# Forty-eight products of ones among the early steps, k as the first transfer, and softmax sums in a PSUM tile of their own

## The chip, the cores and the metric

The kernel runs on one core of one Trainium2 chip. The metric is the device time of one execution in microseconds (us). Timed runs of the kernel before gave 588.23, 587.32 and 587.64, median 587.64.

The engines are TensorE (PE, with its weight loads as PEld), VectorE (DVE), ScalarE (ACT) and GpSimd (POOL). SyncE (SP) issues all transfers from HBM. Each engine works through its own list in order; between engines there are semaphores.

## The reference

Attention of 4 batches, 8 heads, 768 positions and a head dimension of 64: each query sees the keys within 15 positions and one summary for each block of 32 keys (the maximum of its keys, the mean of its values). Its output goes through an MLP from 512 to 2048 and back, with an exact gelu.

```python
k_sum = k.reshape(B, H, nb, block, D).max(axis=3)
v_sum = v.reshape(B, H, nb, block, D).mean(axis=3)
scores_l = scale * np.matmul(q, k.transpose(0, 1, 3, 2))
scores_l_m = np.where(mask_l, scores_l, -1000000000.0)
scores_s = scale * np.einsum('bhsd,bhnd->bhsn', q, k_sum) + np.log(block)
scores_all = np.concatenate([scores_l_m, scores_s], axis=-1)
a = np.exp(scores_all - np.max(scores_all, axis=-1, keepdims=True))
a = a / (np.sum(a, axis=-1, keepdims=True) + 1e-09)
attn_out = np.matmul(a, np.concatenate([v, v_sum], axis=2))
x = attn_out.transpose(0, 2, 1, 3).reshape(B * S, H * D)
h = x @ w_in
out = (0.5 * h * (1.0 + erf(h / np.sqrt(2.0)))) @ w_out
```

The weights are drawn in 64-bit and come in as raw 64-bit words.

## The kernel before

The attention is cut into 24 units of 4 heads and 256 queries; two units make a chunk of 256 tokens with all 512 columns of x. Units 0 to 5 compute in f32, the later ones in f16 with a high and a low part. Chunks 0 and 1 go through `phase1` (x times w_in, three f16 products for each) and `phase2` (times w_out); from chunk 2 on groups of chunks share sums and differences, so that fewer products are needed.

What every engine does, and in which order, stands in one string, `ORDER`: some 1,670 named steps, each with its numbers. The program goes through it and issues each step's instructions; every engine gets its part in this order, and the transfers of the `fetch_` and `load_` steps go to SP in this order too. The string is at the head of the file; its first line names the steps of the first microseconds.

The steps that matter here, with their lines in the trace:

- `setup` (L325): GpSimd sets constants; `ones` is 128 x 64 of 1.0. TensorE multiplies `ones` with itself 16 times (`N_FILL`, L331) into a tile of the pool `ps_h` that nobody reads.
- `fetch_k 0 g` (L496) brings k for two pairs of heads of batch 0 (784 KB); `prep_k` (L505) takes the block maxima on VectorE, `prep_k_end` (L513, L514) splits them, `k_pack` (L633, L635) lays k and the maxima out on ScalarE.
- `load_q u` (L577) brings q of unit u into the only q tile. The first in the string is that of unit 6, which `s_q_hi` (ScalarE, L682) and `q_lo` (VectorE, L691) split at once; `load_q 0` has to wait until they have read it.
- `f_mask` (L620) writes the mask into the scores' tile by f16 products, `f_scores` (L649) adds q times k in f32, `evac` (ScalarE, L727) copies the scores, `maximum` (GpSimd, L740) takes the maximum over partitions, `m_shift` (L697) subtracts it by products with one row, `m_exponent` (ScalarE, L703) applies the exponential. The scores have one PSUM tile (`ps_s`, two banks), so the next unit's `f_mask` waits for `m_exponent`.
- `f_sums` (L671) sums the exponentials by products with ones, `norm_take` (VectorE, L814) transposes the sums out of PSUM, `norm_cross` (ScalarE, L822, L827), `norm_rec` (L830) and `norm_spread` (L834) make the factors. `f_values` (L663) multiplies with v, `norm_mult` (VectorE, L841) applies the factors, `x_hi` (L845) and `x_lo` (L848) split x for the MLP. Sums and values share one tile of two banks, `psv`: values in its first bank, sums in its second. There is one such tile, and waits are kept for a tile as a whole. `sums` and `values` are the f16 forms of the later units.
- `fetch_w_in`, `wi_bits` (L372, L377, L381), `wi_hi` (ScalarE, L407), `wi_lo` (VectorE, L410) and `wt_add` turn the 64-bit words of w_in into f16 parts. `sum_vt` (L532) and `mean_vt` make the means of v for batch 0.
- `phase1 c i` (L868 to L870): 24 products for chunk c and 256 columns i of w_in, into a tile of `ps_h` (three tiles).

Of the kernel before, what the change touches and what calls it, by code (L numbers as in the profile page):

```python
# [77 lines left out]
sum_vt 0, wi_bits 5 0, wt_add 3 1, wt_add 3 2, wi_lo 3, load_v 0, wi_hi 2, wt_hi 3, evac 1, maximum 1, fetch_vt 2,
wi_bits 5 1, wt_lo 3, load_q 2, sum_vt 1, norm_take 0, norm_cross 0, k_pack 2, m_shift 1, m_exponent 1, sum_vt 2,
norm_rec 0, norm_spread 0, wi_bits 6 0, wi_bits 5 2, wi_bits 6 1, wi_lo 2, wi_hi 5, mean_vt, s_load_vs 0, wi_bits 6 2,  # L80
fetch_w_in 4 4, wi_lo 5, f_mask 2, f_scores 2, evac 2, wi_bits 4 0, wi_bits 4 1, maximum 2, load_v 1, s_load_vs 1,
f_values 0, norm_mult 0, x_hi 0, fetch_w_in 0 0, k_pack 3, f_sums 1, norm_take 1, x_lo 0, load_v 2, norm_cross 1,
wi_bits 4 2, m_shift 2, load_q 3, f_values 1, wi_bits 0 0, m_exponent 2, norm_rec 1, norm_spread 1, f_mask 3,
norm_mult 1, wi_bits 0 1, wi_hi 4, f_scores 3, fetch_w_in 1 1, x_hi 1, x_lo 1, wi_bits 0 2, wi_bits 1 0, evac 3,
fetch_v 1 1, f_sums 2, phase1 0 3, wi_hi 0, wi_hi 6, norm_take 2, fetch_w_in 7 3, wi_bits 1 1, load_k 4, wi_lo 6,
load_vs 2, prep_v 1 1, f_values 2, fetch_k 1 3, norm_cross 2, phase1 0 2, k_sums 0 0, norm_rec 2, norm_spread 2,
phase1 0 5, load_v 3, wi_bits 1 2, fetch_k 1 1, gelu 0 3, norm_mult 2, maximum 3, m_shift 3, wi_hi 1, load_v 4,
m_exponent 3, wi_lo 0, prep_k 1 3, phase1 0 6, gelu 0 5, wi_lo 1, wi_bits 7 0, load_vs 3, prep_k 1 1, f_sums 3,
norm_take 3, wi_bits 7 1, fetch_k 1 2, x_hi 2, f_values 3, load_q 4, prep_k 1 2, gelu 0 2, g_hi 0 3, fetch_v 1 2, g_lo
0 3, g_hi 0 2, norm_cross 3, norm_rec 3, g_hi 0 5, phase1 0 0, x_lo 2, k_pack 4, fetch_k 1 0, norm_spread 3, norm_mult  # L90
3, x_hi 3, phase1 0 1, gelu 0 1, fetch_v 1 0, wi_bits 7 2, g_lo 0 5, g_hi 0 1, x_lo 3, load_vs 4, f_mask 4, f_scores
4, wi_hi 7, evac 4, gelu 0 6, prep_k 1 0, maximum 4, wi_lo 7, phase1 1 3, prep_v 1 2, f_mask 5, prep_v 1 0, g_lo 0 2,
g_hi 0 6, gelu 1 3, g_lo 0 1, g_lo 0 6, load_k 5, fetch_w_out 1 5, wo_bits 1 0, k_pack 5, shift 4, fetch_w_out 0 4,
load_k 6, phase1 1 7, g_hi 1 3, wo_bits 1 1, phase1 0 7, gelu 1 7, g_hi 1 7, g_lo 1 7, exponent 4, wo_bits 1 2, gelu 0
7, wo_bits 0 0, wo_bits 0 1, wo_bits 0 2, load_q 5, phase1 1 1, gelu 0 0, g_hi 0 0, f_sums 4, g_hi 0 7, f_values 4,
gelu 1 1, wo_hi 1, g_lo 0 0, norm_take 4, f_scores 5, norm_cross 4, g_lo 0 7, phase1 1 6, g_hi 1 1, evac 5, wo_lo 1,
gelu 1 6, s_k_hi 6, fetch_w_out 3 5, wi_lo 4, norm_rec 4, load_q 7, load_v 6, phase1 1 2, norm_spread 4, norm_mult 4,
fetch_w_out 2 4, g_lo 1 3, phase1 1 4, maximum 5, wo_hi 0, wo_lo 0, f_mask 6, gelu 1 2, phase1 1 5, load_mask, k_lo 6,
fetch_v 1 3, shift 5, load_v 5, exponent 5, prep_k_end 1 0, load_k 8, wo_bits 3 0, g_lo 1 1, wo_bits 3 1, phase1 1 0,
gelu 1 0, g_hi 1 2, prep_v 1 3, wo_bits 3 2, phase2 0 0, g_hi 1 6, k_sums 1 0, load_vs 5, gelu 1 5, g_hi 1 5, f_sums  # L100
5, wo_hi 3, wo_bits 2 0, g_lo 1 2, norm_take 5, wo_bits 2 1, phase1 0 4, s_q_hi 7, x_hi 4, wo_bits 2 2, wo_hi 2, wo_lo
3, load_vs 6, q_lo 7, scores 6, s_k_hi 8, wo_lo 2, prep_k_end 1 1, fetch_w_out 5 5, f_values 5, k_sums 0 1, k_lo 8,
x_lo 4, phase2 0 1, norm_cross 5, evac 6, maximum 6, norm_rec 5, norm_spread 5, norm_mult 5, fetch_w_out 4 4, phase2 0
3, gelu 1 4, wo_bits 5 0, v_hi 6, wo_bits 5 1, f_mask 7, x_hi 5, x_lo 5, g_hi 1 4, g_lo 1 4, gelu 0 4, g_lo 1 5,
phase2 0 2, phase1 2 4, wo_bits 4 0, g_lo 1 6, gelu 2 4, phase1 2 1, wo_bits 4 1, wo_bits 4 2, load_v 8, load_k 7,
s_k_hi 7, phase1 2 0, g_hi 0 4, wo_hi 4, gelu 2 1, load_q 8, wo_bits 5 2, wo_hi 5, shift 6, wo_lo 4, load_vs 8, phase1
2 2, fetch_w_out 7 5, g_hi 1 0, g_lo 0 4, wo_lo 5, s_q_hi 8, gelu 2 0, g_lo 1 0, phase2 0 4, exponent 6, s_p_hi 6,
k_lo 7, phase1 2 6, v_lo 6, fetch_w_out 6 4, k_sums 1 1, scores 7, q_lo 8, v_hi 8, p_lo 6, gelu 2 6, sums 6, wo_bits 7
0, wo_bits 6 0, wo_bits 7 1, load_k 9, wo_bits 6 1, wo_bits 6 2, values 6, s_k_hi 9, evac 7, phase2 0 5, phase1 2 7,
wo_bits 7 2, wo_hi 6, wo_lo 6, wo_hi 7, fetch_k 2 3, load_q 9, g_hi 2 0, load_v 7, load_vs 7, wo_lo 7, k_lo 9, scores  # L110
8, norm_take 6, add_mask 8, phase2 0 6, norm_cross 6, norm_rec 6, norm_spread 6, s_q_hi 9, g_hi 2 1, phase2 0 7, store
0 0, maximum 7, v_lo 8, q_lo 9, shift 7, exponent 7, s_p_hi 7, phase2 1 0, norm_mult 6, load_q 11, s_q_hi 11, phase2 1
2, g_hi 2 4, phase2 1 4, wt_add 4 0, put 0 0, prep_k 2 3, p_lo 7, sums 7, v_hi 7, store 0 1, fetch_v 2 0, v_lo 7,
wt_add 4 1, wt_add 4 2, load_v 9, put 0 1, load_k 11, load_vs 9, g_lo 2 4, g_hi 2 6, norm_take 7, g_lo 2 1, g_lo 2 0,
prep_v 2 0, maximum 8, x_hi 6, phase2 1 6, gelu 2 2, phase1 2 5, norm_cross 7, norm_rec 7, x_lo 6, store 1 0, shift 8,
scores 9, gelu 2 7, q_lo 11, exponent 8, values 7, fetch_v 2 2, wt_hi 4, phase2 1 1, norm_spread 7, wt_lo 4, phase2 1
3, phase2 1 5, add_mask 9, prep_v 2 2, norm_mult 7, load_q 10, phase2 1 7, load_v 11, g_hi 2 2, s_q_hi 10, s_p_hi 8,
s_k_hi 11, load_vs 11, p_lo 8, sums 8, values 8, v_hi 9, v_lo 9, maximum 9, shift 9, fetch_k 2 1, k_lo 11, prep_k 2 1,
g_hi 2 7, g_lo 2 7, scores 11, exponent 9, put 1 0, x_hi 7, phase1 2 3, norm_take 8, load_k 10, x_lo 7, phase1 3 7,
g_lo 2 6, q_lo 10, gelu 2 5, load_v 10, add_mask 11, norm_cross 8, norm_rec 8, fetch_k 2 2, s_p_hi 9, norm_spread 8,  # L120
p_lo 9, s_k_hi 10, phase1 3 5, gelu 2 3, norm_mult 8, store 1 1, gelu 3 5, prep_k 2 2, prep_k_end 2 1, sums 9,
norm_take 9, x_hi 8, phase2 2 1, k_lo 10, scores 10, fetch_k 2 0, put 1 1, values 9, maximum 11, g_hi 2 3, g_lo 2 3,
g_hi 2 5, norm_cross 9, shift 11, exponent 11, wt_add 5 0, s_p_hi 11, load_vs 10, load_k 12, norm_rec 9, norm_spread
9, phase1 3 4, load_q 12, s_q_hi 12, g_lo 2 5, gelu 3 7, v_hi 10, phase1 3 0, gelu 3 4, v_hi 11, g_hi 3 4, norm_mult
9, g_lo 2 2, phase2 2 3, x_hi 9, wt_add 1 0, phase1 3 3, wt_add 1 1, wt_add 1 2, p_lo 11, g_hi 3 5, q_lo 12, wt_hi 1,
add_mask 10, sums 11, gelu 3 3, v_lo 11, g_hi 3 3, prep_k 2 0, phase2 2 5, load_v 12, g_lo 3 4, fetch_v 2 1, phase1 3
6, norm_take 11, wt_add 5 1, norm_cross 11, g_lo 3 3, k_sums 2 1, prep_k_end 2 0, k_sums 2 0, load_q 13, gelu 3 0,
s_q_hi 13, wt_lo 1, s_k_hi 12, q_lo 13, k_lo 12, wt_add 5 2, wt_hi 5, phase1 3 1, prep_v 2 1, v_lo 10, phase2 2 7,
store 2 1, scores 12, load_k 13, wt_lo 5, phase1 3 2, maximum 10, shift 10, wt_add 0 0, values 11, s_k_hi 13, load_q
14, s_q_hi 14, phase2 2 0, phase2 2 2, wt_add 2 0, g_hi 3 0, norm_rec 11, norm_spread 11, exponent 10, s_p_hi 10,  # L130
norm_mult 11, g_lo 3 0, phase2 2 4, g_lo 3 5, wt_add 0 1, p_lo 10, values 10, wt_add 2 1, wt_add 0 2, x_lo 8, wt_hi 0,
# [1165 lines left out]
```

## Time and profile before

| | us |
|---|---|
| median of three runs | 587.64 |
| lowest and highest | 587.32 and 588.23 |
| the profiled execution's own time | 588.54 |
| its span, first to last instruction | 586.8 |
| TensorE busy (share of the span) | 568.8 (97%) |
| VectorE busy | 459.2 (78%) |
| ScalarE busy | 386.5 (66%) |
| GpSimd busy | 87.5 (15%) |

The span is that of the instructions; 1.7 us of the profiled execution's time lie around it. Busy time is the union of an engine's instructions. Matmuls overlap in the array and their ends are modelled, so a busy TensorE need not be one at its peak. The granted clock is the share of TensorE's 2.4 GHz that it was allowed in a stretch; it has two levels here, 0.50 and 1.00.

### The profile page before, as it was taken

How to read it: one execution, taken by the hardware profiler on the slowest of the kernel's cores; microseconds unless marked ns; L12 is line 12 of the kernel's file. 1: busy time of each engine (PE TensorE's matmuls, PEld its weight loads, DVE VectorE, ACT ScalarE, POOL GpSimd, SP SyncE). 2: the span in 40 equal slices, each digit the busy share in tenths (PEclk: the TensorE clock that was granted, in tenths of full speed). 3: DMA queues.
4: the chain of work that ended last, by engine and by line, in shares of the span. 5: the costliest groups of instructions: out<-in, count | busy, mean ns of one | idle time of the engine just before them, and what ended most of it. 6: DMA issues, size and time to landing. Idle time of an engine off the chain costs nothing.

```text
span 586.8 us, 13450 instructions
## 1 busy us (share of the span) xinstructions
PE 568.8 (97%) x5784; PEld 392.8 (67%) x5784; DVE 459.2 (78%) x621; ACT 386.5 (66%) x648; POOL 87.5 (15%) x42
## 2 busy tenths in 40 slices
...
GB/s 290 328 245 279 165 209 292 194 168 131 147 146 167 82 42 159 100 116 121 75 85 75 85 133 4 56 99 79 74 62 1 20 19 19 1 18 2 2 1 91
DMA packets 28652, 64.27 MB, mean 110 GB/s; under 512 B 2736, under 2 KB 7600, under 8 KB 28592
## 3 DMA queue, kind: packets, MB, share of 16 engines
...
q8 instruction: 45, 0.74, 0.5%
...
## 4 chain that ended last, share of the span: by engine, by line
PE 92%; ACT 2%; POOL 2%; DMA 2%; DVE 2%; issue 1%; POOLq 0%; DVEq 0%; ACTq 0%
PE psy L939 13%; PE pso L987 12%; PE pso L989 11%; PE pso L988 11%; PE psz L939 7%; PE psh L868 5%; PE psh L869 5%; PE psh L870 5%; PE pso_y L1152 4%; PE psx L939 3%; PE pss L649 3%; PE psv L793 3%; PE pss L716 2%; PE pss_x L1152 2%; POOL m L740 2%; DMA q<-in_qd_dram 2%
## 5 line engine op out<-in xcount | busy, mean ns | idle before, releaser
L740 POOL PARTITION_ALL_REDUCE m<-s x24 | 81.3, 3386 | 331.9 <-DVE s L731 113.0
L987 PE MATMUL pso<-w_out_h,gg 128*128 128x512 f16 x320 | 121.5, 380 | 0.0
L988 PE MATMUL pso<-w_out_l,gg 128*128 128x512 f16 x320 | 121.3, 379 | 0.0
L989 PE MATMUL pso<-w_out_h,gg 128*128 128x512 f16 x320 | 121.3, 379 | 0.0
L939 PEld LDWEIGHTS <-wt 128*128 128x128 f16 x768 | 74.5, 98 | 13.6 <-issue 0.8
L868 PE MATMUL psh<-xos,ww 128*128 128x256 f16 x256 | 70.9, 277 | 0.0
L869 PE MATMUL psh<-xos,ww 128*128 128x256 f16 x256 | 70.8, 277 | 0.0
L870 PE MATMUL psh<-xos,ww 128*128 128x256 f16 x256 | 70.8, 276 | 0.0
L939 PE MATMUL psy<-xos,wt 128*128 128x256 f16 x576 | 69.3, 273 | 0.0
L939 PEld LDWEIGHTS <-ww 128*128 128x128 f16 x576 | 55.1, 98 | 11.8 <-issue 0.6
L989 PEld LDWEIGHTS <-gg 128*128 128x128 f16 x320 | 31.3, 98 | 37.8
L987 PEld LDWEIGHTS <-gg 128*128 128x128 f16 x320 | 31.3, 98 | 33.7 <-issue 1.5
L988 PEld LDWEIGHTS <-gg 128*128 128x128 f16 x320 | 31.3, 98 | 31.6
L950 ACT ACTIVATE ww<-psy 128x512 f32<-128x512 f32 x48 | 28.1, 590 | 31.1 <-PE psy L939 30.8
L971 DVE SCALAR_TENSOR_TENSOR gg<-g,gg 128x512 f16<-128x512 f32 x48 | 34.8, 731 | 13.4 <-ACT gg L967 13.4
L957 DVE TENSOR_TENSOR g<-psz,ww 128x512 f32<-128x512 f32 x24 | 16.4, 685 | 20.3 <-PE psz L939 17.6
L967 ACT ACTIVATE gg<-g 128x512 f16<-128x512 f32 x48 | 29.3, 623 | 3.2 <-PE pso L988 2.6
L877 ACT ACTIVATE g<-psh 128x512 f32<-128x512 f32 x32 | 18.8, 594 | 16.8 <-PE psh L870 14.5
L868 PEld LDWEIGHTS <-ww 128*128 128x128 f16 x256 | 25.4, 99 | 6.2 <-issue 2.0
L964 ACT ACTIVATE g<-g 128x512 f32<-128x512 f32 x36 | 22.2, 622 | 8.8 <-DVE g L957 8.8
L869 PEld LDWEIGHTS <-ww 128*128 128x128 f16 x256 | 25.4, 99 | 3.8
L870 PEld LDWEIGHTS <-ww 128*128 128x128 f16 x256 | 25.4, 99 | 3.3
...
## 6 DMA issues: line engine op xcount, KB each, us to landing
...
```

The costliest lines, as they stand in the source:

```text
L740: nc.gpsimd.partition_all_reduce(out_ap=self.m32, in_ap=self.s32, channels=P, reduce_op=bass_isa.ReduceOp.max)
L868: nc.tensor.matmul(ph[:, e, :], wh, xh, start=(k == 0), stop=False)
L869: nc.tensor.matmul(ph[:, e, :], wh, xl, start=False, stop=False)
L870: nc.tensor.matmul(ph[:, e, :], wl, xh, start=False, stop=(k == NCC - 1))
L939: nc.tensor.matmul(ps[:, e, :], ws, xx, start=(first and e == 0 and k == 0 and m == 0), stop=(k == 1 and m == 2), skip_group_check=True,)
L950: nc.scalar.activation(snaps[b, q, n], split8(acc[b, q, "y"]), AF.Copy)
L967: nc.scalar.activation(g_part(o // 2, q, 0, slice(o % 2, 4, 2)), g32t[b, q, o], AF.Copy, scale=SC_G)
L971: nc.vector.scalar_tensor_tensor(out=g_part(o // 2, q, 1, fs), in0=g32t.pop((b, q, o)), scalar=SC_G, in1=g_part(o // 2, q, 0, fs), op0=ALU ...
L987: nc.tensor.matmul(p, gh, w_out_h[:, f, :], start=(f == 0), stop=False)
L988: nc.tensor.matmul(p, gh, w_out_l[:, f, :], start=False, stop=False)
L989: nc.tensor.matmul(p, gl, w_out_h[:, f, :], start=False, stop=(f == NFC - 1))
L1152: nc.tensor.matmul(ps[:, j, :], g, ww_, start=(first and e == 0 and k == 0), stop=(e == 1 and k == 2), skip_group_check=True,)
```

## The change

Four things are changed; the order of all other steps stays.

A new step `fill k` multiplies `ones` with itself six times into a tile of `ps_h` of its own, as `setup` does 16 times. Eight such sets stand in the string: 7 and 0 behind `f_mask 0`, 4, 3, 2 and 1 behind `f_scores 0`, 6 and 5 behind `f_sums 1`. `fetch_k 0 0` moves from the fifth place of the string to the first, ahead of `load_q 6`. The tile of two banks for values and sums is parted: values get a tile of one bank (`ps_v`), sums one of half a bank (`ps_d`), each with waits of its own. `v_tile` makes a new tile at each call instead of reusing the unit's.

```diff
+N_FILL_STEP = 6
...
-load_q 6, s_q_hi 6, q_lo 6, load_m16, fetch_k 0 0, prep_k 0 0, fetch_w_in 3 3, f_mask 0, load_q 0, prep_k_end 0 0,
+fetch_k 0 0, load_q 6, s_q_hi 6, q_lo 6, load_m16, prep_k 0 0, fetch_w_in 3 3, f_mask 0, fill 7, fill 0, load_q 0,
...
+    ps_d = ctx.enter_context(tc.tile_pool(name="ps_d", bufs=1, space=PSUM))
...
+    def products_of_ones(name, n):
+        t = ps_h.tile([P, DM], F32, tag="psh", name=f"psh_fill_{name}")
+        for _ in range(n):
+            nc.tensor.matmul(
+                t[:D].rearrange("p (n d) -> p n d", d=D), ones, ones.unsqueeze(1).broadcast_to([P, DM // D, D]),
+                start=True, stop=True,
+            )
+
+    def fill(k):
+        products_of_ones(k, N_FILL_STEP)
...
-            self.pss = self.psv = None
+            self.pss = None
...
-                            self.psv[e * D : (e + 1) * D, 0, col], v[:, vo : vo + D], self.s32[:, po : po + TQ],
+                            self.psv[e * D : (e + 1) * D, col], v[:, vo : vo + D], self.s32[:, po : po + TQ],
...
         def f_sums(self):
-            self.v_tile()
+            self.d_tile()
...
-                    self.psv[i * 32 : (i + 1) * 32, 1, :CH], ones_f, self.s32[:, i * CH : (i + 1) * CH],
+                    self.psd[i * 32 : (i + 1) * 32], ones_f, self.s32[:, i * CH : (i + 1) * CH],
...
         def v_tile(self):
-            if self.psv is None:
-                self.psv = ps_v.tile([P, 2, NR * CH], F32, tag="psv", name=f"psv_{self.nm}")
+            self.psv = ps_v.tile([P, NR * CH], F32, tag="psv", name=f"psv_{self.nm}")
+
+        def d_tile(self):
+            self.psd = ps_d.tile([P, CH], F32, tag="psd", name=f"psn_{self.nm}")
...
-            nc.vector.transpose(out=self.dent[:, :CH], in_=self.psv[:, 1, :CH])
+            nc.vector.transpose(out=self.dent[:, :CH], in_=self.psd)
```

On SP, at the program's start, before: q of unit 6, the mask, k, the bits of w_in 3, q of unit 0.

```order
L577 DMA q_6_123<-in_qd_dram 128x512
L317 DMA mask_sb<-in_mask_dram 128x320
L496 DMA w_out_l<-in_kp_dram 128x2x784
L357 DMA gg<-in_w_in_dram 128x4x512
L577 DMA q_0_138<-in_qd_dram 128x512
```

The same now (`w_out_l` is the room in which k waits).

```order
L504 DMA w_out_l<-in_kp_dram 128x2x784
L585 DMA q_6_127<-in_qd_dram 128x512
L319 DMA mask_sb<-in_mask_dram 128x320
L365 DMA gg<-in_w_in_dram 128x4x512
L585 DMA q_0_155<-in_qd_dram 128x512
```

k moved ahead of q of unit 6 and of the mask; w_in 3 and q of unit 0 keep their places.

On TensorE around the scores of unit 0, before: the last product of the mask, the 16 score products, the shift by the maximum, the mask of unit 1.

```order
L620 MATMUL pss_133<-mask_sb 128x2x192
L649 MATMUL pss_133<-q_0_138,kf_143 128x64 x16
L697 MATMUL pss_133<-m_0_179,neg_77 128x512 x2
L620 LDWEIGHTS mask_sb
L620 MATMUL pss_192<-mask_sb 128x2x64
```

The same now, of each set of six products the first row.

```order
L628 MATMUL pss_136<-mask_sb 128x2x192
...
L331 MATMUL psh_fill_141<-ones 64x512
...
L331 MATMUL psh_fill_148<-ones 64x512
...
L657 MATMUL pss_136<-q_0_155,kf_160 128x64 x16
...
L331 MATMUL psh_fill_179<-ones 64x512
...
L331 MATMUL psh_fill_186<-ones 64x512
...
L331 MATMUL psh_fill_193<-ones 64x512
...
L331 MATMUL psh_fill_200<-ones 64x512
...
L705 MATMUL pss_136<-m_0_224,neg_80 128x512 x2
```

Two sets came in ahead of the scores and four between the scores and the shift.

On TensorE around the sums of unit 1, before: values of unit 0 and sums of unit 1 (tile `psv`), the shift of unit 2, values of unit 1.

```order
L663 MATMUL psv_215<-s_0_177,v_0_227 64x64 x16
L671 MATMUL psv_320<-s_1_231,ones_f 32x256 x4
L697 MATMUL pss_270<-m_2_293,neg_77 128x512 x2
L663 MATMUL psv_320<-s_1_231,v_1_295 64x64 x16
L620 LDWEIGHTS mask_sb
```

The same now, with the sums in a tile `psn`.

```order
L671 MATMUL psv_343<-s_0_222,v_0_272 64x64 x16
L679 MATMUL psn_366<-s_1_276,ones_f 32x256 x4
...
L331 MATMUL psh_fill_371<-ones 64x512
...
L331 MATMUL psh_fill_378<-ones 64x512
...
L705 MATMUL pss_315<-m_2_338,neg_80 128x512 x2
L671 MATMUL psv_401<-s_1_276,v_1_340 64x64 x16
```

Two sets came in ahead of the shift of unit 2, and the sums no longer write the tile of the values.

## Rows read from the trace of the kernel before

**Rows 1.** Stretches: length, busy us (instructions) by engine, granted clock, DMA share, GB/s

```profile
11.70:32.17 20.47, 14.72 (x85) 9.23 (x86) 16.31 (x19) 9.25 (x15) 6.58 (x2) 0.50 0.90 319
32.17:45.83 13.66, 10.94 (x123) 5.79 (x121) 12.25 (x15) 9.09 (x15) 4.76 (x2) 1.00 0.71 262
45.83:56.07 10.24, 10.14 (x68) 7.06 (x65) 8.13 (x10) 6.98 (x14) 0.00 (x0) 0.50 0.88 309
56.07:100.00 43.93, 43.31 (x488) 36.77 (x487) 40.84 (x50) 33.61 (x54) 12.35 (x5) 1.00 0.66 215
100.00:583.00 483.00, 482.90 (x5008) 330.97 (x5006) 377.92 (x525) 324.14 (x548) 62.46 (x19) 1.00 0.25 79
```

**Rows 2.** Timeline, TensorE, to 52 us: start, us, what [idle before <-releaser]

```profile
11.55 3.58 PE L649 MATMUL pss<-q,kf 64*128 64x64 f32 x32 [4.51 <-DMA q<-in_qd_dram]
19.70 2.07 PE L697 MATMUL pss<-m,neg 1*128 1x512 f32 x4 [4.57 <-POOL m L740]
22.96 1.01 PE L620 MATMUL pss<-mask_sb 128*128 128x128 f16 x4 [1.18 <-ACT s L703]
23.90 3.68 PE L649 MATMUL pss<-q,kf 64*128 64x64 f32 x32
27.51 1.08 PE L671 MATMUL psv<-s,ones_f 128*32 128x256 f32 x8
28.52 5.46 PE L532 MATMUL psh_vt<-w_out_h,w_out_l 128*88 128x512 f32 x8
...
34.97 1.95 PE L532 MATMUL psh_vt<-w_out_h,w_out_l 128*88 128x512 f32 x4
...
37.28 2.00 PE L649 MATMUL pss<-q,kf 64*128 64x64 f32 x32
...
41.16 0.64 PE L671 MATMUL psv<-s,ones_f 128*32 128x256 f32 x8 [0.79 <-DVE x32s L841]
43.73 1.13 PE L697 MATMUL pss<-m,neg 1*128 1x512 f32 x4 [1.93 <-POOL m L740]
...
46.98 3.68 PE L649 MATMUL pss<-q,kf 64*128 64x64 f32 x32
```

**Rows 3.** Timeline, the other engines and weight loads, to 20 us

```profile
3.49 0.63 ACT L682 ACTIVATE qh<-q 128x512 f16<-128x512 f32 x1 [1.47 <-DMA q<-in_qd_dram]
...
4.35 0.18 PEld L331 LDWEIGHTS <-ones 128*64 128x64 f16 x1 [0.25 <-issue]
4.78 1.24 PEld L331 LDWEIGHTS <-ones 128*64 128x64 f16 x6 [0.25 <-issue]
...
8.05 0.74 ACT L633 ACTIVATE kf<-w_out_l 128x640 f32<-128x640 f32 x1 [3.93 <-DMA w_out_l<-in_kp_dram]
...
10.76 0.69 DVE L372 TENSOR_SCALAR wt<-gg 128x1024 int32<-128x1024 int32 x1 [0.50 <-DMA gg<-in_w_in_dram]
...
14.01 1.06 ACT L407 ACTIVATE ww<-wt 128x1024 f16<-128x1024 f32 x1 [3.69 <-DVE wt L381]
...
16.29 3.35 POOL L740 PARTITION_ALL_REDUCE m<-s  x1 [14.31 <-ACT s L727]
```

**Rows 4.** Timeline, VectorE, 26 to 75 us: its waits, and x_lo of unit 1

```profile
28.66 0.45 DVE L814 STREAM_TRANSPOSE dent<-psv 128x256 f32<-128x256 f32 x1 [2.61 <-PE psv L671]
...
41.87 0.45 DVE L814 STREAM_TRANSPOSE dent<-psv 128x256 f32<-128x256 f32 x1 [0.76 <-PE psv L671]
...
47.73 0.68 DVE L848 TENSOR_TENSOR xos<-x32s,xos 128x512 f16<-128x512 f32 x1
...
51.74 0.45 DVE L814 STREAM_TRANSPOSE dent<-psv 128x256 f32<-128x256 f32 x1 [1.59 <-PE psv L671]
...
67.40 0.45 DVE L814 STREAM_TRANSPOSE dent<-psv 128x256 f32<-128x256 f32 x1 [1.82 <-PE psv L671]
```

**Rows 5.** Timeline, TensorE, 55 to 70 us

```profile
56.49 1.15 PE L663 MATMUL psv<-s,v 128*64 128x64 f32 x32
...
67.96 1.15 PE L663 MATMUL psv<-s,v 128*64 128x64 f32 x32 [0.62 <-issue]
```

More of the change, by code (lines that the diff above doesn't have):

```diff
@@ L78 @@
[L78 to L131, printed above, removed]
-add_mask 12, gelu 3 6, g_hi 3 6, sums 10, gelu 3 2, fetch_v 2 3, wt_lo 0, x_lo 9, prep_v 2 3, sp 2 1 1, norm_take 10,
@@ new lines @@
+maximum 2, load_v 1, s_load_vs 1, f_values 0, norm_mult 0, x_hi 0, fetch_w_in 0 0, k_pack 3, f_sums 1, fill 6, fill 5,
+norm_take 1, x_lo 0, load_v 2, norm_cross 1, wi_bits 4 2, m_shift 2, load_q 3, f_values 1, wi_bits 0 0, m_exponent 2,
+norm_rec 1, norm_spread 1, f_mask 3, norm_mult 1, wi_bits 0 1, wi_hi 4, f_scores 3, fetch_w_in 1 1, x_hi 1, x_lo 1,
+wi_bits 0 2, wi_bits 1 0, evac 3, fetch_v 1 1, f_sums 2, phase1 0 3, wi_hi 0, wi_hi 6, norm_take 2, fetch_w_in 7 3,
+wi_bits 1 1, load_k 4, wi_lo 6, load_vs 2, prep_v 1 1, f_values 2, fetch_k 1 3, norm_cross 2, phase1 0 2, k_sums 0 0,
@@ new lines @@
+norm_rec 2, norm_spread 2, phase1 0 5, load_v 3, wi_bits 1 2, fetch_k 1 1, gelu 0 3, norm_mult 2, maximum 3, m_shift
+3, wi_hi 1, load_v 4, m_exponent 3, wi_lo 0, prep_k 1 3, phase1 0 6, gelu 0 5, wi_lo 1, wi_bits 7 0, load_vs 3, prep_k
+1 1, f_sums 3, norm_take 3, wi_bits 7 1, fetch_k 1 2, x_hi 2, f_values 3, load_q 4, prep_k 1 2, gelu 0 2, g_hi 0 3,
+fetch_v 1 2, g_lo 0 3, g_hi 0 2, norm_cross 3, norm_rec 3, g_hi 0 5, phase1 0 0, x_lo 2, k_pack 4, fetch_k 1 0,
+norm_spread 3, norm_mult 3, x_hi 3, phase1 0 1, gelu 0 1, fetch_v 1 0, wi_bits 7 2, g_lo 0 5, g_hi 0 1, x_lo 3,
@@ new lines @@
+4, wo_bits 2 2, wo_hi 2, wo_lo 3, load_vs 6, q_lo 7, scores 6, s_k_hi 8, wo_lo 2, prep_k_end 1 1, fetch_w_out 5 5,
+f_values 5, k_sums 0 1, k_lo 8, x_lo 4, phase2 0 1, norm_cross 5, evac 6, maximum 6, norm_rec 5, norm_spread 5,
+norm_mult 5, fetch_w_out 4 4, phase2 0 3, gelu 1 4, wo_bits 5 0, v_hi 6, wo_bits 5 1, f_mask 7, x_hi 5, x_lo 5, g_hi 1
+4, g_lo 1 4, gelu 0 4, g_lo 1 5, phase2 0 2, phase1 2 4, wo_bits 4 0, g_lo 1 6, gelu 2 4, phase1 2 1, wo_bits 4 1,
+wo_bits 4 2, load_v 8, load_k 7, s_k_hi 7, phase1 2 0, g_hi 0 4, wo_hi 4, gelu 2 1, load_q 8, wo_bits 5 2, wo_hi 5,
@@ new lines @@
+s_q_hi 9, g_hi 2 1, phase2 0 7, store 0 0, maximum 7, v_lo 8, q_lo 9, shift 7, exponent 7, s_p_hi 7, phase2 1 0,
+norm_mult 6, load_q 11, s_q_hi 11, phase2 1 2, g_hi 2 4, phase2 1 4, wt_add 4 0, put 0 0, prep_k 2 3, p_lo 7, sums 7,
+v_hi 7, store 0 1, fetch_v 2 0, v_lo 7, wt_add 4 1, wt_add 4 2, load_v 9, put 0 1, load_k 11, load_vs 9, g_lo 2 4,
+g_hi 2 6, norm_take 7, g_lo 2 1, g_lo 2 0, prep_v 2 0, maximum 8, x_hi 6, phase2 1 6, gelu 2 2, phase1 2 5, norm_cross
+7, norm_rec 7, x_lo 6, store 1 0, shift 8, scores 9, gelu 2 7, q_lo 11, exponent 8, values 7, fetch_v 2 2, wt_hi 4,
```

262 lines of the change are left out of this document (146 added, 116 removed).

## The prediction, made before the changed kernel ran

> **What bounds the kernel now.** The first view to read is the table of stretches. From 100 us to 583 TensorE is busy for 482.90 of 483.00 us at a granted clock of 1.00 (its 2.4 GHz level), and from 56.07 to 100 for 43.31 of 43.93 [rows 1]: behind 56 us there is nothing to win but work that TensorE is spared, and the change spares it none there. Ahead of 56 us it is different. The granted clock is 0.50 (1.2 GHz) from 11.70 to 32.17 and again from 45.83 to 56.07, 30.7 us in all, and TensorE is idle for about a quarter of the first of these [rows 1]. So whatever lets TensorE begin `phase1` (51.6 us in this trace: 46.98 + 3.68 + 1.08, less 0.1 of overlap [rows 2]) and leave it sooner comes off the end one for one, as long as what VectorE and ScalarE make for it comes forward too.
>
> The second view is TensorE's timeline of these 56 us [rows 2]. The reader should follow one chain: scores of unit 0 (L649, at 11.55), a wait of 4.57 us for the maximum on GpSimd, `m_shift` (L697), a wait for the exponential that frees the scores' PSUM tile, then mask, scores of unit 1, its sums and the eight products of `sum_vt` (L620, L649, L671, L532) without a gap from 22.96 to 33.98, and so on to unit 3 at 46.98. The same lines stand there at both levels: L649 takes 3.58 and 3.68 at half clock and 2.00 at full, L671 1.08 and 0.64, L697 2.07 and 1.13.
>
> The third view is the start on the other engines [rows 3]. The 16 products of ones at the start begin 0.43 us apart (4.35, 4.78) and then 0.21 (six in 1.24): they raise the clock, and one costs 0.43 at half and 0.21 at full. The clock fell at 11.70 after TensorE had had nothing to do since 7.0 (11.55 less the 4.51 idle before it), rose at 32.17 within the dense products of `sum_vt`, and fell at 45.83 after some 4 us that held only an `m_shift` of 1.13 and `f_values` [rows 1, 2].
>
> **The first transfer.** Now the engines start on q of unit 6 at 3.49, on k of the first two units at 8.05 and on the bits of w_in 3 at 10.76, each as soon as it has landed [rows 3]. With k first, q lands behind it. The three transfers together stay the same bytes, so q lands somewhere between 3.49 and 8.05; I take 7.2, because k is issued first and the row of 8.05 is the last of them. Then `s_q_hi` (0.63) and `q_lo` (about the same) end at 8.6, and only then is the q of unit 0 issued on SP, which is held by that wait; queued behind it there are w_in 2, the second k and w_in 5. A transfer of this size at the head of the queue was there 3.49 after the span's start, so q of unit 0 lands by 12.1 at the latest if it is as quick; since the first transfer can't have been issued at 0, I take 11.5, as now (11.55). `prep_k` stands behind `q_lo` on VectorE, so k's earlier landing starts nothing earlier; it ends at about 10.8 and VectorE begins on w_in 3 at 10.8 instead of 10.76. Value taken: 0. Ends: nothing gained, because VectorE waits for w_in 3 in any case, and 0.9 lost, if q lands at 8.05.
>
> **Unit 0 and its 36 products.** Twelve products (2.5 us at full clock) fall into the 4.51 us before the scores of unit 0 and keep the clock up. These scores then take 2.0 instead of 3.58. That alone buys almost nothing: `evac 0` stands on ScalarE behind `wi_hi 3` (L407), which ends at 15.07 because VectorE needs until 14.0 for w_in 3 [rows 3]. So the maximum is ready 0.1 earlier, at 19.6, and `m_shift` then takes 1.13 instead of 2.07. Together **-1.0**. The 24 products behind the scores cost 24 x 0.21 = 5.1 and have the 4.57 of the wait and the 1.6 that the scores got shorter: covered, with 1.0 to spare.
>
> **Units 1 and `sum_vt`.** The chain from 22.96 to 33.98 is 11.0 at half clock (1.01 + 3.68 + 1.08 + 5.46, less their overlaps). At full clock it is 0.5 + 2.0 + 0.64 + twice the 1.95 that four products of L532 take, 7.0, with 0.2 of gaps 7.2: -3.8 if the clock holds, 0 if not. Between the last of the 24 products (18.6) and the scores of unit 1 (22) TensorE has only `m_shift` and a mask. That is nearest to the row at 43.73, after which the clock fell. I take a fall part of the way through this chain: **-2.5**.
>
> **Unit 2 to `phase1`.** Scores of unit 2 ran at full clock already. `f_sums 1` no longer waits for `norm_mult 0` (0.79, L841), because sums have their own tile; with the 1.93 of the wait for GpSimd that is 2.7 us, into which the last twelve products (2.5) just fit. Scores of unit 3 then take 2.00 instead of 3.68 and its sums 0.64 instead of 1.08: **-2.1**. `phase1 0 3` runs from 51.6 to 56.49 [rows 5], 4.9 for 24 products at half clock; at full it is 2.4. I take a third of that, **-0.8**, because the stretch from `m_shift 2` to its start is thin again.
>
> **The tiles.** `f_values 3` at 67.96 starts 0.62 after the sums, which it follows only because the transpose has to read the shared tile first [rows 5]: **-0.6**. Other waits of this kind hardly show in 100 to 583 [rows 1], so I take nothing there.
>
> **What VectorE gives back.** These parts make -7.0. VectorE makes weights and x for TensorE, and it can come forward only by the idle time it has: 2.61 at 28.66, 0.76 at 41.87, 1.59 at 51.74, 1.82 at 67.40, together 6.8, of which 5.0 by the time `phase1` runs [rows 4]. The x of unit 1 is ready at 48.41 now (L848), so `phase1` at 51.6 - 5.6 = 46.0 needs it 2.3 earlier, which the first two of these cover. Later TensorE is ahead of VectorE by about 1 us more than now; I take back 0.7. Sum **-6.3**. The profiled execution took 588.54 us (span 586.8 and 1.7 around it), so it becomes 582.2. The median of the runs, 587.64, is 0.9 lower; on it the forecast is **581.3**.
>
> **Rivals.** (A) The clock holds everywhere: -1.0 - 3.8 - 2.1 - 2.4 - 0.6 = -9.9, held back by VectorE's 6.8 of idle time and whatever it has made ahead; half way, -8.4, gives 579.2. For it: the products are as dense as those that raised the clock at the start. Against: the thin stretches around `m_shift`. (B) The clock falls before unit 1 and again before unit 3: -1.0 - 0.6 - 0.8 = -2.4, 585.2. For it: the fall at 45.83 after a stretch of the same make-up.
>
> (C) Slower: the 24 products run at half clock because it was not up when they began. They then cost 10.3 against a cover of 4.57 and hold back `m_shift 0` by 5.7; the last twelve cost 5.2 against 2.7, 2.5 more; less 0.6 that is +7.6, 595.2. It decides at the granted clock under the first of the 24, and it needs that clock to stay at 0.50 through all of them. Against it: products of the same kind raised it within 4 us at the start.
>
> (D) The change does not do what it says: the products do not hold the clock, and only the tiles help: 587.0, within what a measurement of this kernel can tell from no change (about 0.2%, 1.2 us).
>
> (E) All half clock comes back. The rows show 30.7 us at 0.50, of which TensorE was busy 14.7 + 10.1 [rows 1]. If the whole stretch were TensorE's own work, half of it, 15.4, would go: 572.3. Against: 1 us in 5 of it is waiting, and VectorE has only 6.8 to give.
>
> [...]
>
> **How the numbers follow.** Forecast (580.0 to 583.6) 0.52, A 0.22, B 0.15, D 0.05, C 0.04, E 0.02. Faster by over 0.2% are the forecast, A, B and E: 0.91; D is 0.05, C 0.04. The range leaves out C, D, E and the outer parts of A and B: 578.7 to 585.4.
>
> **What would show it.** Right: a granted clock of 1.00 under the scores of units 0 and 3; `m_shift 0` still at about 19.6; `evac 0` still behind `wi_hi 3`; `phase1` from about 46; VectorE's idle time before its transposes mostly gone. The first step is wrong if VectorE begins on w_in 3 later than 11. Unit 1 is wrong by the granted clock from 22 to 30. The prediction falls if the 24 products end after the maximum of unit 0, or if TensorE shows new waits on VectorE or ScalarE between 56 and 130 us that eat the lead.

## The result, and the profile after

The changed kernel took 580.17 us in the median of four runs (578.46 to 581.40), the kernel before 587.48 in four: a ratio of 0.9885, 95% interval 0.9838 to 0.9932, so 6.8 us (4.0 to 9.5) less. In a second series it took 581.23 (579.77 to 582.04, six runs) against 587.00, ratio 0.9912 (0.9887 to 0.9937). The forecast was 581.3, from 578.7 to 585.4.

| | before | after |
|---|---|---|
| median of the runs, us | 587.48 | 580.17 |
| the profiled execution's own time | 588.54 | 578.46 |
| its span | 586.8 | 576.7 |
| TensorE busy (share of the span) | 568.8 (97%) | 569.7 (99%) |
| mean granted clock, as a share of full speed | 0.974 | 0.996 |

The profiled execution of the changed kernel is the fastest of its ten; the other nine had a mean clock of 0.990 to 0.994. So its trace shows what the change does when most goes well, and the experiments below show the usual case.

First the stretches of the profiled execution, cut where the granted clock changes (columns as in [rows 1]: length, busy us of TensorE, its weight loads, VectorE, ScalarE, GpSimd, granted clock, DMA share, GB/s):

```profile
5.51:22.58 17.07, 15.11 (x114) 8.64 (x114) 15.73 (x19) 7.27 (x10) 3.65 (x1) 1.00 0.99 358
22.58:25.99 3.41, 3.41 (x19) 1.32 (x18) 2.20 (x4) 2.67 (x8) 1.43 (x1) 0.50 1.03 409
25.99:56.00 30.01, 29.30 (x301) 19.13 (x300) 28.25 (x34) 20.76 (x34) 11.87 (x6) 1.00 0.86 288
```

At half clock TensorE spends 3.41 us between the first rise of the clock (5.51) and 56 us, against the 20.47 + 10.24 of [rows 1]. The traces give the clock as a share and not in GHz; what they show of the two levels is a rate: products of ones with 512 columns start 0.426 us apart at half clock (eight steps from 0.94 to 4.35 in the kernel before) and 0.216 at full (12 take 2.78 and 24 take 5.37 here), which is 1.2 and 2.4 columns in a ns.

The timeline of TensorE that answers to [rows 2]; of `phase1` only its first product stands here:

```profile
7.29 2.78 PE L331 MATMUL psh_fill<-ones 128*64 128x512 f16 x12
10.16 2.00 PE L657 MATMUL pss<-q,kf 64*128 64x64 f32 x32
12.09 5.37 PE L331 MATMUL psh_fill<-ones 128*64 128x512 f16 x24
18.14 1.13 PE L705 MATMUL pss<-m,neg 1*128 1x512 f32 x4 [0.69 <-POOL m L748]
20.46 0.60 PE L628 MATMUL pss<-mask_sb 128*128 128x128 f16 x4 [1.18 <-ACT s L711]
20.98 2.26 PE L657 MATMUL pss<-q,kf 64*128 64x64 f32 x32
23.17 1.08 PE L679 MATMUL psn<-s,ones_f 128*32 128x256 f32 x8
24.18 4.55 PE L540 MATMUL psh_vt<-w_out_h,w_out_l 128*88 128x512 f32 x8
...
35.61 2.78 PE L331 MATMUL psh_fill<-ones 128*64 128x512 f16 x12
39.00 1.13 PE L705 MATMUL pss<-m,neg 1*128 1x512 f32 x4 [0.61 <-POOL m L748]
...
41.83 2.00 PE L657 MATMUL pss<-q,kf 64*128 64x64 f32 x32
43.76 0.64 PE L679 MATMUL psn<-s,ones_f 128*32 128x256 f32 x8
44.33 0.28 PE L878 MATMUL psh<-xos,ww 128*128 128x256 f16 x1
```

The 24 products ended 0.69 ahead of the maximum; the scores of units 0 and 3 took 2.00 each; `phase1` began at 44.33 instead of 51.60. From there to the end of the span it is 532.37 us (576.7 - 44.33), before it was 535.2 (586.8 - 51.60). So 7.3 of the 10.1 us were won ahead of `phase1`, and 2.8 in it and behind it.

The other engines, answering to [rows 3] (ScalarE, then VectorE):

```profile
5.74 0.63 ACT L690 ACTIVATE qh<-q 128x512 f16<-128x512 f32 x1 [3.73 <-DMA q<-in_qd_dram]
...
12.38 1.06 ACT L415 ACTIVATE ww<-wt 128x1024 f16<-128x1024 f32 x1 [3.11 <-DVE wt L389]
13.35 1.00 ACT L735 ACTIVATE s<-pss 128x1024 f32<-128x1024 f32 x1
```

```profile
9.14 0.69 DVE L380 TENSOR_SCALAR wt<-gg 128x1024 int32<-128x1024 int32 x1
```

VectorE began on the bits of w_in 3 at 9.14, not at 10.76, and without a wait. The waits of VectorE that [rows 4] show ahead of its transposes (2.61, 0.76, 1.59, 1.82) are gone in this profile; in that of `after_again`, the same kernel, 1.76 of the first is there. What is left on VectorE between 20 and 75 us:

```profile
25.98 0.25 DVE L840 RECIPROCAL rc<-rc 128x16 f32<-128x16 f32 x1 [1.21 <-ACT rc L837]
41.25 0.69 DVE L851 TENSOR_TENSOR x32s<-psv,dent 128x512 f32<-128x512 f32 x1 [0.45 <-PE psv L671]
45.74 0.70 DVE L380 TENSOR_SCALAR wt<-gg 128x1024 int32<-128x1024 int32 x1 [0.92 <-DMA gg<-in_w_in_dram]
62.03 0.25 DVE L840 RECIPROCAL rc<-rc 128x16 f32<-128x16 f32 x1 [0.86 <-ACT rc L837]
```

And `f_values 3`, where [rows 5] had an idle time of 0.62:

```profile
57.84 1.15 PE L671 MATMUL psv<-s,v 128*64 128x64 f32 x32
```

### The profile page after: what moved, and what is told of

Same layout as the page of the kernel before. It is cut to its first block, busy times and chain, and to the rows that moved or that the text cites. A ratio compares the mean times of both kernels' runs of the same rounds, so it can differ in the third digit from the quotient of the medians.

```text
span 576.7 us, 13547 instructions
## 1 busy us (share of the span) xinstructions
PE 569.7 (99%) x5832; PEld 391.5 (68%) x5832; DVE 456.9 (79%) x621; ACT 386.2 (67%) x648; POOL 88.3 (15%) x42
## 4 chain that ended last, share of the span: by engine, by line
PE 91%; DVE 2%; ACT 2%; POOL 2%; DMA 1%; issue 1%; SPq 0%; POOLq 0%; DVEq 0%; ACTq 0%
PE psy L949 13%; PE pso L997 12%; PE pso L998 12%; PE pso L999 12%; PE psz L949 7%; PE psh L878 5%; PE psh L880 5%; PE psh L879 5%; PE pso_y L1162 4%; PE psx L949 3%; PE psv L801 3%; PE pss L724 2%; POOL m L748 2%; PE pss_x L1162 2%; PE pss L657 2%; PE psh_vt L540 1%
## 5 line engine op out<-in xcount | busy, mean ns | idle before, releaser
L748 POOL PARTITION_ALL_REDUCE m<-s x24 | 82.5, 3439 | 320.3 <-DVE s L739 112.9
L878 PE MATMUL psh<-xos,ww 128*128 128x256 f16 x256 | 69.9, 273 | 0.0
L880 PE MATMUL psh<-xos,ww 128*128 128x256 f16 x256 | 69.8, 273 | 0.0
L879 PE MATMUL psh<-xos,ww 128*128 128x256 f16 x256 | 69.8, 273 | 0.0
L949 PEld LDWEIGHTS <-ww 128*128 128x128 f16 x576 | 55.1, 98 | 11.8 <-issue 0.6
L878 PEld LDWEIGHTS <-ww 128*128 128x128 f16 x256 | 25.0, 98 | 5.5 <-issue 1.6
L1004 ACT ACTIVATE ot<-pso 128x512 f32<-128x512 f32 x20 | 11.8, 592 | 23.7 <-PE pso L999 23.6
L879 PEld LDWEIGHTS <-ww 128*128 128x128 f16 x256 | 25.1, 98 | 3.5
```

The costliest lines, as they stand in the source:

```text
L748: nc.gpsimd.partition_all_reduce(out_ap=self.m32, in_ap=self.s32, channels=P, reduce_op=bass_isa.ReduceOp.max)
L878: nc.tensor.matmul(ph[:, e, :], wh, xh, start=(k == 0), stop=False)
L879: nc.tensor.matmul(ph[:, e, :], wh, xl, start=False, stop=False)
L880: nc.tensor.matmul(ph[:, e, :], wl, xh, start=False, stop=(k == NCC - 1))
L949: nc.tensor.matmul(ps[:, e, :], ws, xx, start=(first and e == 0 and k == 0 and m == 0), stop=(k == 1 and m == 2), skip_group_check=True,)
```

## The experiments

Each was timed in several rounds beside the kernel before, the twelve in three series of four. The last three columns come from the one profiled execution of each: the time at half clock between 5 and 57 us, the start of `phase1`, and the span. Executions of one kernel scatter by up to 5 us, and their mean granted clock goes with it (the kernel before, first series: from 588.31 at 0.974 to 583.58 at 0.982), so medians decide, and a single profile only tells how.

| label | median, us (before beside it) | ratio, 95% | half clock | phase1 | span |
|---|---|---|---|---|---|
| k_first | 585.97 (587.17) | 0.9982 (0.9959 to 1.0004) | 30.7 | 50.29 | 585.4 |
| tiles | 586.99 (587.17) | 1.0002 (0.9981 to 1.0024) | 20.5 | 48.67 | 581.0 |
| fills | 581.92 (587.17) | 0.9918 (0.9888 to 0.9948) | 6.8 | 47.04 | 580.0 |
| k_tiles | 585.39 (587.17) | 0.9968 (0.9947 to 0.9989) | 27.3 | 49.91 | 584.1 |
| after_again | 581.23 (587.00) | 0.9912 (0.9887 to 0.9937) | 10.2 | 46.73 | 580.3 |
| no_70 | 580.45 (587.00) | 0.9904 (0.9879 to 0.9928) | 10.2 | 46.20 | 578.6 |
| no_4321 | 581.49 (587.00) | 0.9918 (0.9895 to 0.9942) | 13.7 | 47.35 | 579.7 |
| no_65 | 582.89 (587.00) | 0.9951 (0.9930 to 0.9973) | 13.7 | 48.23 | 581.2 |
| more | 582.17 (586.24) | 0.9928 (0.9899 to 0.9956) | 3.4 | 46.55 | 578.9 |
| only65 | 581.82 (586.24) | 0.9924 (0.9898 to 0.9950) | 17.1 | 47.42 | 579.8 |
| no_k | 580.87 (586.24) | 0.9905 (0.9875 to 0.9936) | 6.8 | 46.99 | 579.3 |
| evac | 583.50 (586.24) | 0.9939 (0.9917 to 0.9962) | 10.2 | 47.42 | 581.7 |

### One part alone

`k_first` is the kernel before with the first transfer changed:

```diff
-load_q 6, s_q_hi 6, q_lo 6, load_m16, fetch_k 0 0, prep_k 0 0, ...
+fetch_k 0 0, load_q 6, s_q_hi 6, q_lo 6, load_m16, prep_k 0 0, ...
```

> The kernel before with one edit: k is the first transfer. By the prediction's step the move is worth nothing: VectorE begins on the bits of w_in 3 at 10.8, the shift of unit 0 stays at 19.7, the time stays between 0 and +0.9 us. The rival, read from the trace of the changed kernel (VectorE on w_in 3 at 9.14 instead of 10.76): the move lets the early transfers run closer together, w_in 3 is there at about 9.1, the shift of unit 0 starts at about 18.1, and the time falls by 1 to 1.6 us even without the products.

Measured -1.2 us, with an interval that takes in no change. In its profile VectorE began on w_in 3 at 9.37 and the shift of unit 0 stood at 18.44, near the rival's numbers and not the prediction's. `tiles` has only the PSUM tiles parted, without products, k in fifth place:

```diff
-            self.psv = ps_v.tile([P, 2, NR * CH], F32, tag="psv", ...)
+            self.psv = ps_v.tile([P, NR * CH], F32, tag="psv", ...)
+            self.psd = ps_d.tile([P, CH], F32, tag="psd", ...)
```

> The kernel before with one edit: sums and values in tiles of their own, no products, k in fifth place. By the prediction -0.6 us (the values of unit 3 start without a gap behind its sums, the sums of unit 1 without the 0.79 wait for VectorE). The rival: these waits are taken up by the next one, and the time stays within 0.2 us.

Measured -0.2, interval from -1.1 to +1.4: not to be told from nothing. Its profiled execution (582.80) was the fastest of its 13. `fills` has only the eight sets of products:

```diff
+... f_mask 0, fill 7, fill 0, ...
+... f_scores 0, fill 4, fill 3, fill 2, fill 1, ...
+... f_sums 1, fill 6, fill 5, ...
```

> The kernel before with one edit: the eight sets of six products, k in fifth place, one tile for sums and values. By the prediction -5.7 us (all of its sum but the tiles): scores of unit 0 at full clock, shift of unit 0 at about 19.6, scores of unit 3 at full clock, phase1 from about 46.5. The last twelve products stand behind the sums of unit 1, which here still wait 0.8 for VectorE, so up to 0.5 of them may stick out. The rival, that the earlier k carries part of the gain: -4 to -5 us, and VectorE still begins on w_in 3 at 10.8.

Measured -5.3 (4.8 by the ratio), so the products carry most of the gain. The forecast of -5.7 and the rival's -4 to -5 lie too near each other for this to decide between them. `k_tiles` is the changed kernel without them:

```diff
-... fill 7, fill 0, ... fill 4, fill 3, fill 2, fill 1, ... fill 6, fill 5, ...
```

> The changed kernel without the eight sets of products: k first and tiles of their own remain. By the prediction -0.6 (to +0.3) us against the kernel before, and a granted clock of 0.50 from about 11 on, as before. The rival that the earlier k is worth 1.6 by itself: -1.5 to -2.2 us.

Measured -1.8, as the rival has it, and 1.6 under `tiles`: k first is worth about that much as long as there are no products. How it works is seen on VectorE, at the first instruction on the bits of w_in 3. Before, [rows 3] have it at 10.76; in the other kernels with k in fifth place it is this line (timelines of `tiles`, `fills` and `no_k`, in this order):

```profile
9.56 0.69 DVE L379 TENSOR_SCALAR wt<-gg 128x1024 int32<-128x1024 int32 x1 [0.49 <-DMA gg<-in_w_in_dram]
```

```profile
9.88 0.69 DVE L384 TENSOR_SCALAR wt<-gg 128x1024 int32<-128x1024 int32 x1 [0.61 <-DMA gg<-in_w_in_dram]
```

```profile
10.59 0.69 DVE L380 TENSOR_SCALAR wt<-gg 128x1024 int32<-128x1024 int32 x1 [0.51 <-DMA gg<-in_w_in_dram]
```

It waits for the transfer each time, and the transfer comes at another time in each execution. In the ten profiles with k first it stands between 9.14 and 9.37, with no wait in any. The stretch from 3 to 9 us (its last number is GB/s), before and after:

```profile
3.00:9.00 6.00, 4.04 (x16) 1.68 (x14) 1.65 (x2) 1.37 (x2) 0.00 (x0) 1.00 0.92 277
```

```profile
3.00:9.00 6.00, 6.00 (x24) 2.65 (x23) 2.54 (x3) 1.40 (x3) 0.00 (x0) 1.00 1.00 360
```

277 GB/s became 360 in these two. Over all profiles the kernels with k in fifth place moved 277 to 342 GB/s in this stretch and those with k first 345 to 366, so at its nearest the difference is small. Why the queue ran denser with k first wasn't tried apart.

### One part taken away

`after_again` is the changed kernel itself, for a comparison within the series.

> The changed kernel once more, beside the three that follow. Expected 579 to 581 us, with a fall of the granted clock between 18 and 28 us that is one or two steps long (3.4 or 6.8 us, as in the trace of the changed kernel and of the products alone), and VectorE on the bits of w_in 3 at 9.2 with no wait ahead of it.

Measured 581.23, just above the range. Its profile is that of its slowest execution (582.04): the clock fell at 19.66 and stayed down for 10.24 us, longer than expected, and VectorE began on w_in 3 at 9.30 without a wait.

`no_70` leaves out the two sets ahead of the scores of unit 0, `no_4321` the four behind them, `no_65` the two behind the sums of unit 1, `only65` the first six:

```diff
-... f_mask 0, fill 7, fill 0, load_q 0, ...
...
-... f_scores 0, fill 4, fill 3, fill 2, fill 1, fetch_w_in 2 2, ...
...
-... f_sums 1, fill 6, fill 5, norm_take 1, ...
```

> The changed kernel without sets 7 and 0, the twelve products ahead of the scores of unit 0. If these hold the clock for the scores, as the prediction has it, the clock falls before 12.4 and the 24 products behind the scores begin at half clock: in the worst case 24 x 0.43 = 10.3, the shift of unit 0 at about 24 instead of 18.1, and 3 to 6 us lost against the changed kernel. Rival: the scores and the first products of the 24 bring the clock back within 4 us, most of the lost time is covered by the wait for the maximum, and the loss is under 1 us.

> The changed kernel without sets 4 to 1, the 24 products behind the scores of unit 0. By the prediction's reckoning TensorE is idle from 12.1 to 18.1, the clock is at 0.50 under the shift and through the chain to the end of sum_vt, 0.9 + 2.5 to 3.8 are lost: 583.5 to 585 us. Rival: the chain is at half clock for half of its length anyway in the changed kernel (22.6 to 26.0), and only 1 to 2 us are lost.

> The changed kernel without sets 6 and 5, the twelve products behind the sums of unit 1. By the prediction the clock falls before the scores of unit 3, which then take 3.68 instead of 2.00 and their sums 1.08 instead of 0.64, and phase1 begins at half clock: +2.1 to +2.9 us. Rival: in the trace with the tiles alone the clock was back at 46.49 within the scores of unit 3, so the loss is 0.5 to 1.5 us.

> The changed kernel with sets 6 and 5 alone (no products around the scores of unit 0). Taken away one group at a time, 7 and 0 cost nothing and 4 to 1 cost 0.3. If the two groups stand in for each other, the six sets together are worth 1 to 2 us: 582.5 to 583 us. If they are worth nothing together either, 581 to 581.5, and then sets 6 and 5, k first and the tiles carry the whole gain. The prediction's own terms for these sets (unit 0 and unit 1) say 3.5: 584.5.

Measured against `after_again`: `no_70` -0.8, `no_4321` +0.3, `no_65` +1.7. So `no_70` came out as its rival has it, `no_4321` lost less than either case, and `no_65` lies between prediction and rival, as `only65` does between its two cases. `only65` belongs to another series; its ratio of 0.9924 is 0.0012 above that of `after_again`, 0.7 us, and inside its interval. So the 36 products around the scores of unit 0 bring about 0.7 us between them once the last twelve are there, which these runs don't tell from nothing. The last twelve bring 1.7 (`no_65` against `after_again`) to 2.6 (the ratio of `only65`, 0.0044 under that of `k_tiles`). Such steps from one series to another are rough: the changed kernel's own ratio was 0.9885 in one and 0.9912 in another, 1.6 us apart.

`no_70` also shows what 24 products do when the clock falls 0.2 us after the first of them began, nearly the condition of rival C (its stretches, then TensorE's timeline):

```profile
12.11:15.53 3.42, 3.42 (x9) 1.42 (x8) 3.10 (x5) 2.12 (x3) 1.05 (x1) 0.50 1.04 409
15.53:22.35 6.82, 5.64 (x36) 2.81 (x34) 6.72 (x9) 2.97 (x4) 2.84 (x1) 1.00 0.93 323
```

```profile
11.90 7.05 PE L331 MATMUL psh_fill<-ones 128*64 128x512 f16 x24
18.88 1.13 PE L705 MATMUL pss<-m,neg 1*128 1x512 f32 x4
```

The clock fell at 12.11 and was back at 15.53, under the products themselves. They took 7.05 instead of 5.37, and the shift of unit 0 came 0.6 later than in `after_again` (18.26). Nothing of that reached the end.

What `only65` does is seen in its stretches:

```profile
12.36:29.42 17.06, 9.63 (x51) 5.48 (x52) 12.70 (x16) 8.34 (x14) 5.68 (x2) 0.50 0.94 343
29.42:56.00 26.58, 26.12 (x279) 17.11 (x278) 25.75 (x31) 19.16 (x32) 10.76 (x5) 1.00 0.82 294
```

17 us at half clock remain, but TensorE is busy for only 9.63 of them; from 29.42 on the clock stays up, under the scores of unit 3 and all of `phase1`. In `no_65` it is the other way round, the clock falls at 42.75:

```profile
42.75:49.58 6.83, 6.74 (x49) 4.67 (x48) 5.27 (x7) 3.65 (x5) 0.00 (x0) 0.50 1.01 305
```

Here TensorE is busy for 6.74 of 6.83 us at half clock: nothing else is waited for, and the work itself is late.

`no_k` is the changed kernel with k back in fifth place:

```diff
-fetch_k 0 0, load_q 6, s_q_hi 6, q_lo 6, load_m16, prep_k 0 0, ...
+load_q 6, s_q_hi 6, q_lo 6, load_m16, fetch_k 0 0, prep_k 0 0, ...
```

> The changed kernel with k back in the fifth place. The prediction's step says 0 (a gain of up to 0.9 by going back). From the traces with k first (VectorE on the bits of w_in 3 at 9.14 to 9.37, without a wait) and with k fifth (9.56 to 10.76, with a wait of about 0.5): VectorE begins at 9.6 to 10.8 here, and 0.7 to 1.6 us are lost: 581.8 to 582.8.

The start of VectorE came as expected (10.59), the loss did not: 580.87, ratio 0.9905 against 0.9912 of `after_again`. The shift of unit 0 was at 19.53 instead of 18.26, that of unit 1 at 31.71 instead of 31.58, `phase1` at 46.99 instead of 46.73: the lead is gone by unit 1. The clock fell at 22.98 here and at 19.66 there, so these two profiles don't tell whether the lead was worth nothing or the clock took it back.

### Trying for more

`more` puts a ninth set behind the shift of unit 0, where the clock usually falls:

```diff
-... m_shift 0, prep_k_end 0 1, ...
+... m_shift 0, fill 8, prep_k_end 0 1, ...
```

> The changed kernel with a ninth set of six products behind the shift of unit 0, where TensorE waits 1.18 us for the exponential; six take 1.28 at full clock, so at most 0.1 to 0.2 sticks out. If the thin stretch around this shift is what lets the clock fall between 19.7 and 22.6 in nearly every execution (3.4 to 10 us at 0.50), the fall goes or shrinks, phase1 starts at 44.5 to 45, and the time is 1 to 2 us under the changed kernel's (579 to 580). Rival: the fall comes from the weak products that follow (the mask, scores, sums) and stays, time within 0.5 us of the changed kernel.

The clock held to 31.87 in its profile, but the time did not follow (582.17). The chain ran into GpSimd:

```profile
23.72 0.64 PE L679 MATMUL psn<-s,ones_f 128*32 128x256 f32 x8
24.29 3.67 PE L540 MATMUL psh_vt<-w_out_h,w_out_l 128*88 128x512 f32 x8
29.77 1.13 PE L705 MATMUL pss<-m,neg 1*128 1x512 f32 x4 [1.82 <-POOL m L748]
```

`sum_vt` at full clock ended 1.82 us ahead of the maximum of unit 1, TensorE waited, and the clock fell 2.1 us behind the wait, at 31.87. `evac` lets the copy of unit 0's scores and its maximum go ahead of `wi_hi 3`, and moves set 1 from ahead of the shift of unit 0 to behind it:

```diff
-... load_q 1, wi_hi 3, ... prep_k 0 1, evac 0, maximum 0, fetch_vt 0, m_shift 0, ...
+... load_q 1, evac 0, maximum 0, wi_hi 3, ... prep_k 0 1, fetch_vt 0, m_shift 0, fill 1, ...
```

> The changed kernel with two steps moved: the copy of unit 0's scores and its maximum stand ahead of wi_hi 3 on ScalarE, and set 1 stands behind the shift of unit 0. The prediction says that wi_hi 3 holds this copy; then the copy starts at about 12.2 (when the scores end) instead of 13.4, the shift of unit 0 at 17.0 instead of 18.2, and phase1 0.5 to 1.2 earlier as far as VectorE (idle 0.5 to 1.2 at four places before it) can follow: 579.5 to 580.5, and less if set 1 behind the shift also keeps the clock. Rival: VectorE sets the end of this stretch and the time stays at 581.

The shift of unit 0 did not come earlier in its profile (18.23). The first rise of the clock was late in this execution (7.01), so the products ahead of the scores ended late and the copy began at 12.79; and the maximum, which [rows 3] give 3.35, took longer:

```profile
13.91 4.27 POOL L748 PARTITION_ALL_REDUCE m<-s  x1 [11.92 <-ACT s L735]
```

The clock held to 41.14 all the same, unit 2's shift was at 37.83, 1.2 ahead of the changed kernel's profile, and then this (TensorE, ScalarE, VectorE):

```profile
38.89 1.15 PE L671 MATMUL psv<-s,v 128*64 128x64 f32 x32
41.86 1.01 PE L628 MATMUL pss<-mask_sb 128*128 128x512 f16 x2 [1.82 <-ACT s L711]
42.80 3.68 PE L657 MATMUL pss<-q,kf 64*128 64x64 f32 x32
...
38.16 0.63 ACT L855 ACTIVATE xos<-x32s 128x512 f16<-128x512 f32 x1 [2.71 <-DVE x32s L851]
...
37.45 0.68 DVE L851 TENSOR_TENSOR x32s<-psv,dent 128x512 f32<-128x512 f32 x1
```

TensorE waited for ScalarE, ScalarE for `norm_mult 0` on VectorE, and VectorE had no idle time from 26.05 on. One of its steps ahead of `norm_mult 0` took 2.79 us instead of 1.23 (the last section), and 1.56 earlier would have taken most of the 1.82 from TensorE's wait, had ScalarE's steps behind it moved along. During that wait the clock fell, and the scores of unit 3 and `phase1` ran at half clock. The time was 583.50, with executions from 579.59 (mean clock 0.996) to 584.28 (0.990). No version was found that beats the changed kernel by more than the intervals; `no_70`, which does without twelve of the products, is as fast.

## Why the prediction was right, and where it was not

**The total.** -6.3 was forecast; the medians gave -7.3 in the first series and -5.8 in the second (6.8 and 5.2 by the ratios). That it came so near is partly luck. By the ratios of `k_tiles`, `only65` and `after_again`, k first and the tiles brought 1.9, the last twelve products 2.6 and the first 36 0.7, across three series; the sum had 0.6 for the first of these, 2.9 for the second, and for the third 3.5 less the 0.7 that it took back.

**Unit 3 and `phase1`** (-2.1 and -0.8, together -2.9): right in mechanism, a little large in size. In the profile the scores took 2.00, the sums 0.64, `phase1` ran at full clock, and `fill 6, 5` ended 0.61 ahead of the maximum. The last twelve products measured 1.7 to 2.6.

**Unit 0** (-1.0): the mechanism was right, with one term missing. `evac 0` does stand behind `wi_hi 3` (13.35 behind 12.38 + 1.06), and 24 products fit in (0.69 to spare where 1.0 was forecast). The shift came 1.56 earlier and not 0.1, and that goes with w_in 3, on which VectorE began 1.62 earlier. The shift of unit 0 stands 8.9 to 9.3 us behind that beginning with products or without them: 8.94 in the kernel before, 9.07 in `k_first`, 9.00 in the changed kernel, 8.94 in `no_k` (19.53, 0.17 earlier than before). Of the 13 profiles in which `evac 0` stands behind `wi_hi 3`, only `no_70` has more (9.70). So the products did not bring the shift forward; they only made it shorter (1.13 us instead of 2.07).

**The first transfer** (0): this step failed. The sum assumed that w_in 3 would land when it did, and that q lands at 7.2; q of unit 6 was there at 5.74, w_in 3 by 9.14, and the scores of unit 0, for which q was to land at 11.5, began at 10.16. The sign that was named (VectorE on w_in 3 later than 11) looked only to the other side. A landing was carried over from one trace as if it belonged to the transfer, though it changes with what stands ahead in the queue (there by 9.14 to 9.37 with k first) and differs from run to run (9.56 to 10.76 with k fifth). It mattered little, since VectorE's earlier start is worth 1.2 to 1.6 without the products and nothing that was measured with them (`no_k`). So the 0 came true in the changed kernel, but not for the reason given.

**Unit 1 and `sum_vt`** (-2.5): mis-sized. The part from the mask to the end of the first eight products of `sum_vt` shrank from 11.0 us to 8.3 in the fastest profile (20.46 to 28.73), as forecast. In that of `after_again` the clock fell ahead of the mask, at 19.66, and the same part took 11.1 (20.57 to 31.65):

```profile
20.57 1.01 PE L628 MATMUL pss<-mask_sb 128*128 128x128 f16 x4 [1.18 <-ACT s L711]
...
26.13 5.52 PE L540 MATMUL psh_vt<-w_out_h,w_out_l 128*88 128x512 f32 x8
```

And the six sets that keep the clock up for it and for unit 0 are worth about 0.7 at the end (`only65`). What is won is given back at the next maximum (1.82 in `more`) and to VectorE, whose idle time was used up in `evac`. The prediction took back 0.7 for this. Of the 3.5 that it gave to these sets (2.5 and the 1.0 of unit 0) about 0.7 is left, so some 2 us more than that went. Where they went in the changed kernel itself is read from single profiles and not shown by a run of its own.

**The tiles** (-0.6): the wait of 0.62 is gone, but `tiles` alone gave -0.2 (-1.1 to +1.4), too little to be told apart. A slip without effect: 48.41 less 46.0 is 2.4 us by which the x of unit 1 had to come earlier, not 2.3.

**Behind 56 us.** The new waits that would have sunk the prediction did not show: from 56 to 130 us TensorE is busy for 74.00 of 74.00 us in the changed kernel's profile, and waits 0.91 and 0.19 for ScalarE in that of `after_again`.

**The rivals.** The profiled execution (578.46) comes nearest to case A, though the clock was down for 3.41 us of it; the other nine (579.71 to 582.04, clock 0.990 to 0.994) are at the forecast. C failed twice: in the changed kernel the clock was at 1.00 when the 24 products began (12.09), and in `no_70`, where it fell under them, it was back after 3.42 us. The second fall that B needs, ahead of unit 3, shows in `no_65` and in neither profile of the changed kernel. D is ruled out by `fills`, E by the fastest execution, 6 us above it. E's reckoning, half of the time at half clock, can be held against three pairs of profiles. The changed kernel's was spared 27.3 us of it (30.7 to 3.4), half of which is 13.7, and the span fell by 10.1 (k first and the tiles included). From `k_tiles` to `only65` it is 10.2 us, half 5.1, and the span fell by 4.3; from `only65` to `more` it is 13.7 us, half 6.8, and it fell by 0.9. So the reckoning holds nearly where TensorE was busy without a gap (10.24 of 10.24 us in the stretch from 43.41 that `k_tiles` has and `only65` has not) and not where it waited (9.63 of 17.06 us in that of `only65`). The moment at which the clock changes varies from execution to execution: in the changed kernel's two profiles it first rose at 5.51 and at 6.00, and fell at 22.58 and at 19.66.
